# Second MoE of a fused attention and MoE kernel: early sums of x's quarters, results evacuated to any free slot, the last three in halves

## Chip, cores and metric

One core of one Trainium2 chip runs the whole program. The metric is device time in microseconds, the median of the runs shown; lower is better.

## What is computed

Three stages, each on the output of the one before, all in fp32:

```python
x = attention(q, k, v)                 # 4 x 8 x 576 x 64: downsampled (mean of 4) + banded local, added
x = x.transpose(0, 2, 1, 3).reshape(2304, 512)
h = np.maximum(x @ w_in, 0.0)          # MoE 1: 512 -> 2048 -> 512
x = (s * (h * h) + b) @ w_out
a, c = x @ w_a, x @ w_b                # MoE 2: 512 -> 1536 twice
out = (a * c) @ w_out2                 # 1536 -> 512
```

The change is in MoE 2, for the 2304 tokens that MoE 1 leaves in DRAM (`x2d`).

## The kernel before

Every fp32 operand of TensorE is split into a high and a low part (`hi`: ScalarE copies with rounding to float32r; `lo`: VectorE subtracts), and a product is three matmuls, hi x hi, hi x lo, lo x hi.

MoE 2 runs in three blocks of 768 tokens. A block holds its x transposed in one buffer (`x2`, one buffer, loaded by SyncE at L272) and works as seven products of a Strassen-like scheme on quarters of x (two of four 128-row groups by 384 tokens). The right-hand operands of the products are `B11, T2, B21, T1, T3, B22, T4`: four quarters of x and four sums of quarters, one of which (T3) takes the place of a quarter. `b_x` (L1173) makes them: it forms the sums in place, in the quarters' own memory (`step`, L1194, VectorE, 768 wide), and splits each operand into `xo` (hi L1200 on ScalarE, lo L1203 on VectorE). Because sums overwrite quarters, a sum waits until the operands that read the old content have been split, and the order is a fixed alternation of splits and sums:

```python
        split(0, (0, 0), x2)
        step((0, 1), (1, 1), (0, 1), ALU.subtract, x2)
        step((0, 0), (0, 1), (0, 0), ALU.add, [("xc", t, (0, 1)), ("xo", t, 0)])
```

The operands of the next block can be split only when the products of the last group of the block before have read the old ones. So the seven splits and the sums between them fall at the boundary of two blocks.

For each of six pairs of weight slices, a group computes both tensors' products (TensorE, L1326, `ab<-xo,w`: six 384-wide matmuls each), adds them up on VectorE (L1356, L1369, L1375, L1390, L1400) with one copy on ScalarE (L1350, L1363), and multiplies the two tensors (L1369, L1403) into `u`. `b_out` splits `u` into `gh` (L1442, ScalarE) and `gl` (L1445, VectorE) and multiplies it with the output weights: three 512-wide matmuls for each 128 tokens, hi x hi (L1466), hi x lo (L1467), lo x hi (L1468), into six banks `acc`, each filled over all of a block's groups. `b_comb` makes the weights' operands: hi/lo of slices (L1234, L1237), four sums (L1251), their split (L1268, L1272) and the last quarter's (L1279, L1282). `w_out` splits output weights (L439, L443).

`b_evac` (L1484) moves the six full banks out: ScalarE copies a bank to one of two `ev` buffers (L1490), SyncE writes it to `out` (L1494). With two buffers, an evacuation waits for the transfer of the one before last.

The order of the instructions is set by a planner (`Program.order`, L116 to 217): each task has an engine, an assumed duration, what it reads, the slots it needs (`acq`) and frees (`rel`), and a due time. The task that can start first goes next, and among equals the one due first:

```python
                    key = (s, t.due - t.lead, t.num)
                    if best is None or key < best[0]:
                        best = (key, t, picks, fs)
```

A due time passes backwards from a task to what it needs. `ANY` stands for either of two pools of 128 x 2 x 512 slots (`w`, 33 of them, and `wx`, 4), which weights, sums and temporaries share. A token, such as `("st",)`, limits how many slots one kind of task may hold. Each engine then runs its own instructions strictly in the order written.

Of the kernel before, what the change touches and what calls it, by code (L numbers as in the profile page):

```python
# [55 lines left out]
MAX_STAGED = 4  # L56
NU = max(BLOCKS[0] + 2, *BLOCKS, TN)
# [16 lines left out]
TOKENS = {"ca": 2, "cs": 2, "c2": 2, "st": 1, "wz": 2, "wo": 3, "tt": 6, "gt": 5}  # L74
# [153 lines left out]
def moe_chain(ctx, tc, qT, kT, vd, tq, tk, tv, qu, ku, vu, w_a1, w_o1, w_a2, w_b2, w_o2, sb, ident_d, bmask_d, emask_d, out):  # L228
# [322 lines left out]
    def down(b, hp, ph, pool_eng, v_eng, due=1e9):  # L551
# [170 lines left out]
    def tile_job(i, ph, due):  # L722
# [79 lines left out]
        def e_fn(p):  # L802
            sm = st["sm"] = pools[ph].tile([TQ, 2 * HP], F32, tag="tsm", name="tsm", bufs=3)
# [74 lines left out]
    def unit(u, due):  # L878
# [54 lines left out]
        def sb1(p):  # L933
            st["m"] = pools["b"].tile([128, 2, R], F32, tag="m", name="m", bufs=4)
# [241 lines left out]
    def b_x(t, after):  # L1176
# [31 lines left out]
        x2 = [("x2", t)]
        split(0, (0, 0), x2)
        step((0, 1), (1, 1), (0, 1), ALU.subtract, x2)  # L1210
        step((0, 0), (0, 1), (0, 0), ALU.add, [("xc", t, (0, 1)), ("xo", t, 0)])
        split(1, (0, 0), [("xc", t, (0, 0))])
        split(2, (1, 0), x2)
        step((1, 0), (1, 0), (0, 0), ALU.subtract, [("xc", t, (0, 0)), ("xo", t, 2)])
        P.made["xt1", t] = [last[0]]
        step((0, 0), (1, 1), (0, 0), ALU.subtract, [("xt1", t), ("xo", t, 1)])
        P.made["xt1", t] = [last[0]]
        split(3, (0, 0), [("xt1", t)])
        split(4, (0, 1), [("xc", t, (0, 1)), ("xt1", t)])
        split(5, (1, 1), [("xt1", t)])  # L1220
        split(6, (1, 0), [("xc", t, (1, 0)), ("xt1", t), ("xo", t, 3), ("xo", t, 4), ("xo", t, 5)], end=True)

    def b_comb(g, j):
# [21 lines left out]
        def add2(o, a, b, op):  # L1245
            def fn(picks):
# [4 lines left out]
                V.tensor_tensor(out=s[:, o * half:o * half + half], in0=x, in1=y, op=op)  # L1251
# [402 lines left out]
```

## Time and profile before

| | us |
|---|---|
| median of 3 runs | 943.24 (942.83 to 943.99) |
| profiled execution | 939.76 |
| its span (first to last work) | 937.6 |
| TensorE busy | 913.4 (97%) |
| VectorE busy | 790.3 (84%) |
| ScalarE busy | 498.5 (53%) |
| GpSimd busy | 69.2 (7%) |
| mean granted TensorE clock | 0.993 |

The span is the part of the profiled execution that the engines' records cover; 2.16 us lie around it. Matmuls overlap in the records, since one starts while the last one drains, so a TensorE that is 97% busy has little standstill but may still run at a reduced clock: the granted clock, 1.00 at full speed, tells of that. Each instruction has a start and a length; where the next one on the engine starts before that length is over, the distance of two starts is what an instruction costs. Square brackets at the end of a row give idle time of the engine just before it, and what ended it. MoE 2 fills the time from 505 us on.

### The profile page before, as it was taken

The page shows a single profiled execution, that of the slowest core. Times are in us where ns is not written, and L with a number is a line of the kernel's source. Part 1 is how long each engine was busy: PE and PEld are TensorE (multiplying, and loading weights), DVE is VectorE, ACT ScalarE, POOL GpSimd, SP SyncE. Part 2 cuts the span into 40 slices and gives each one's busy share as a digit, 9 for nine tenths or more (in the row PEclk, how much of TensorE's full clock was granted, in tenths as well). Part 3 has the DMA queues.
Part 4 walks back from the last instruction along what each step waited for, and adds up shares of the span by engine and source line. Part 5 has one row for each costly group of instructions (what it writes and reads, how often), then busy time and mean ns, then how long its engine had stood idle before and what let it go on. Part 6 is the DMA issues. An engine that isn't in the chain of part 4 may idle for free.

```text
span 937.6 us, 14356 instructions
## 1 busy us (share of the span) xinstructions
PE 913.4 (97%) x5319; PEld 847.1 (90%) x5319; DVE 790.3 (84%) x1385; ACT 498.5 (53%) x1144; POOL 69.2 (7%) x70
## 2 busy tenths in 40 slices
PE   8988999999999999999999999999999999999997
PEld 4668989998999999999999999998999998999996
DVE  6998998999999999995977998779877778877753
ACT  3999994445535444445987554335433335433322
POOL 2231201032222200000000000000000000000000
PEclk9998999999999999999999999999999999999999
DMA  7869626234354332304666331103100000300001
GB/s 207 239 180 348 148 72 205 71 102 127 113 103 123 108 88 74 110 15 175 208 213 251 120 113 46 45 23 135 46 23 23 23 23 12 102 31 16 1 1 68
DMA packets 46430, 96.75 MB, mean 103 GB/s; under 512 B 6344, under 2 KB 20520, under 8 KB 45976
## 3 DMA queue, kind: packets, MB, share of 16 engines
q1 hardware_dynamic: 39160, 93.16, 31.0%
q0 software_dynamic: 7200, 2.67, 2.4%
q8 instruction: 42, 0.69, 0.3%
q14 instruction: 28, 0.23, 0.1%
HBM read 83.22 MB, written 12.58 MB: 102 GB/s over the span
## 4 chain that ended last, share of the span: by engine, by line
PE 81%; DVE 8%; ACT 4%; issue 3%; DMA 2%; POOL 1%; SPq 0%; ACTq 0%; POOLq 0%
PE ab L1326 27%; PE acc L1095 6%; PE acc L1096 6%; PE acc L1097 6%; PE h L1052 6%; PE h L1053 6%; PE h L1054 6%; PE acc L1468 5%; PE acc L1467 5%; PE acc L1466 5%; DVE pr L962 1%; DMA pv<-in_vd_dram 1%; DVE xo L1203 1%; DMA tq<-in_bmask_dram 1%; ACT w L342 1%
## 5 line engine op out<-in xcount | busy, mean ns | idle before, releaser
L1326 PE MATMUL ab<-xo,w 128*128 128x384 f32 x1232 | 264.5, 339 | 0.8 <-DVE w L1356 0.5
L1326 PEld LDWEIGHTS ab<-xo,w 128*128 128x128 f32 x1232 | 222.8, 189 | 15.3 <-DVE u L1400 1.0
L1095 PE MATMUL acc<-gh,w 128*128 128x384 f32 (+1 forms) x384 | 134.0, 349 | 4.0 <-ACT w L809 2.0
L1052 PE MATMUL h<-xsh,w 128*128 128x384 f32 x384 | 131.0, 341 | 0.0
L1096 PE MATMUL acc<-gl,w 128*128 128x384 f32 x384 | 130.9, 341 | 0.0
L1097 PE MATMUL acc<-gh,w 128*128 128x384 f32 (+1 forms) x384 | 130.5, 340 | 0.0
L1053 PE MATMUL h<-xsl,w 128*128 128x384 f32 x384 | 128.9, 336 | 0.0
L1054 PE MATMUL h<-xsh,w 128*128 128x384 f32 x384 | 128.9, 336 | 0.0
L1069 ACT ACTIVATE u<-h 128x384 f32<-128x384 f32 x96 | 47.1, 491 | 115.8 <-PE h L1054 114.4
L1442 ACT ACTIVATE gh<-u 128x384 fp32r<-128x384 f32 x68 | 35.7, 525 | 93.4 <-DVE u L1403 58.4
L1095 PEld LDWEIGHTS acc<-gh,w 128*128 128x128 f32 x384 | 73.0, 190 | 8.1 <-ACT w L809 2.6
L1326 PE MATMUL ab<-xo,wx 128*128 128x384 f32 x280 | 77.5, 339 | 0.4 <-DVE u L1369 0.4
L1052 PEld LDWEIGHTS h<-xsh,w 128*128 128x128 f32 x384 | 72.1, 188 | 2.4 <-issue 2.0
L1096 PEld LDWEIGHTS acc<-gl,w 128*128 128x128 f32 x384 | 73.0, 190 | 0.6 <-DVE gl L1080 0.5
L1097 PEld LDWEIGHTS acc<-gh,w 128*128 128x128 f32 x384 | 72.9, 190 | 0.0
L1053 PEld LDWEIGHTS h<-xsl,w 128*128 128x128 f32 x384 | 72.2, 188 | 0.0
L1054 PEld LDWEIGHTS h<-xsh,w 128*128 128x128 f32 x384 | 72.1, 188 | 0.0
L1080 DVE TENSOR_TENSOR gl<-u,gh 128x384 fp32r<-128x384 f32 x96 | 54.4, 566 | 15.2 <-ACT gh L1076 14.9
L1350 ACT ACTIVATE w<-ab 128x384 f32<-128x384 f32 x30 | 14.7, 490 | 91.9 <-PE ab L1326 91.7
L1468 PE MATMUL acc<-w,gl 128*128 128x512 f32 x159 | 62.6, 394 | 0.0
L1467 PE MATMUL acc<-w,gh 128*128 128x512 f32 x159 | 62.6, 393 | 0.0
L1466 PE MATMUL acc<-w,gh 128*128 128x512 f32 x159 | 62.4, 393 | 0.0
(199 smaller groups left out, 1754.3 us busy)
## 6 DMA issues: line engine op xcount, KB each, us to landing
w<-in_w_o_dram SPq DMA_DIRECT2D x28, 512.0 KB
w<-in_w_a_dram SPq DMA_DIRECT2D x25, 512.0 KB
bk<-in_ku_dram SPq DMA_DIRECT2D x22, 320.0 KB
bk<-in_vu_dram SPq DMA_DIRECT2D x22, 320.0 KB
w<-wod SPq DMA_DIRECT2D x12, 512.0 KB
w<-in_w_b_dram SPq DMA_DIRECT2D x11, 512.0 KB
x2d<-ev SPq DMA_DIRECT2D x24, 192.0 KB
x<-x2d SPq DMA_DIRECT2D x3, 1536.0 KB
```

Source lines behind the costliest of these rows:

```text
L1052: nc.tensor.matmul(out=st["h"], lhsT=w[:, 0, k], rhs=hi[:, k], start=(k == 0), stop=False)
L1053: nc.tensor.matmul(out=st["h"], lhsT=w[:, 0, k], rhs=lo[:, k], start=False, stop=False)
L1054: nc.tensor.matmul(out=st["h"], lhsT=w[:, 1, k], rhs=hi[:, k], start=False, stop=(k == HP - 1))
L1069: A_.activation(out=st["u"], in_=st["h"], func=ACTF.Relu)
L1080: V.tensor_tensor(out=st["lo"], in0=st["u"], in1=st["hi"][:, :n].bitcast(F32), op=ALU.subtract)
L1095: nc.tensor.matmul(out=acc, lhsT=wh, rhs=st["hi"], start=(f == 0), stop=False)
L1096: nc.tensor.matmul(out=acc[:, :n], lhsT=wh, rhs=st["lo"], start=False, stop=False)
L1097: nc.tensor.matmul(out=acc, lhsT=wl, rhs=st["hi"], start=False, stop=(f == FA - 1))
L1326: nc.tensor.matmul(out=o, lhsT=w[:, k], rhs=x, start=(not more and k + n == 0), stop=(k == 1 and n == 2), skip_group_check=more,)
L1466: nc.tensor.matmul(out=acc, lhsT=gh, rhs=w[:, 0], start=first, stop=False)
L1467: nc.tensor.matmul(out=acc, lhsT=gh, rhs=w[:, 1], start=False, stop=False)
L1468: nc.tensor.matmul(out=acc, lhsT=gl, rhs=w[:, 0], start=False, stop=last)
```

## The change

First, six small buffers of the attention (`nb`, `sm`, `tnb`, `tsm` and `m` twice) have twice as many copies. Second, the sums of x's quarters: T1, T2 and T4 get slots of their own from `ANY` (a token `xt` allows three), and T3 alone is still made in place. So the sums no longer wait for splits. All are due 15 us ahead of the block, where before they had no due time of their own. Each split names the sums that must be done before its quarter may be given back, and the x buffer is given back when the four quarters that are operands have been split. All sums and all low parts remain on VectorE (`T_ENG`, `X2_ENG`, `S_ENG` name the engine of each). Third, evacuation: a full bank goes to any free slot (token `eva` allows four) in place of the two `ev` buffers. The last block's last three tiles go in halves of 256 columns: ScalarE copies half 0 and SyncE writes it out; VectorE copies half 1 and the DMA for it is issued by ScalarE.

```diff
-TOKENS = {"ca": 2, "cs": 2, "c2": 2, "st": 1, "wz": 2, "wo": 3, "tt": 6, "gt": 5}
+TOKENS = {"ca": 2, "cs": 2, "c2": 2, "st": 1, "wz": 2, "wo": 3, "tt": 6, "gt": 5, "xt": 3, "eva": 4}
...
-            nb = st["nb"] = pools[ph].tile([HK, 4], F32, tag="nb", name="nb", bufs=4)
+            nb = st["nb"] = pools[ph].tile([HK, 4], F32, tag="nb", name="nb", bufs=8)
...
         def step(out, a, b, op, reads):
+
             def fn(p):
-                V.tensor_tensor(out=q(*out), in0=q(*a), in1=q(*b), op=op)
-
-            last[0] = add("DVE", dve(2 * TN), fn, reads, [("xc", t, out)])
...
+                if isinstance(out, str):
+                    st[out] = slot(p[0], F32)
+                eng.tensor_tensor(out=q(out), in0=q(a), in1=q(b), op=op)
+
+            held[out] = add(
+                name, cost(2 * TN), fn, x2 + reads, [("xc", t, out)], [ANY, ("xt",)] if isinstance(out, str) else (), due=due - 15
+            )
+
+        step("T1", (0, 1), (0, 0), ALU.subtract, [])
+        step((0, 1), (1, 1), (0, 1), ALU.subtract, [("xc", t, "T1")])
+        step("T2", (0, 1), (0, 0), ALU.add, [("xc", t, (0, 1))])
+        step("T4", (1, 0), "T2", ALU.subtract, [("xc", t, "T2")])
+        done = []
+        for o, src in enumerate(((0, 0), "T2", (1, 0), "T1", (0, 1), (1, 1), "T4")):
...
+            tl = add(lo_name, lo_cost(2 * TN), lo, [("xh", t, o)], [("xo", t, o)])
+            if isinstance(src, str):
+                tl.rel = [pick(held[src], 0), "xt"]
+            else:
+                done.append(tl)
...
+        add("CTL", 0.0, free_fn, after=done, rel=["xx2"])
...
-        for tt in (3, 4, 5, 0, 1, 2):
-            sv = {}
-
-            def e_fn(p, tt=tt, sv=sv):
-                sv["ev"] = new("", "ev", [128, DM])
-                A_.activation(out=sv["ev"], in_=mm["bacc", t, tt], func=ACTF.Copy)
...
+        for n, tt in enumerate((3, 4, 5, 0, 1, 2)):
+            end = t == len(BLOCKS_B) - 1 and n > 2
             due = target_b((t + 1) * NP, 1.2)
...
+            halves = 2 if end else 1
...
+                    if i:
+                        V.tensor_copy(out=sv["ev"], in_=src)
+                    else:
+                        A_.activation(out=sv["ev"], in_=src, func=ACTF.Copy)
...
+                    (A_ if i else nc.sync).dma_start(out=out[r0:r0 + 128, i * w:i * w + w], in_=sv["ev"])
...
+                te = add(
+                    "DVE" if i else "ACT", dve(w) if i else act(w, True), e_fn, [("bacc", t, tt)], [("bev", t, tt, i)],
+                    [ANY, ("eva",)], (), due,
+                )
+                add("ACT" if i else "SP", 0.1 if i else 0.73, s_fn, [("bev", t, tt, i)], rel=[pick(te, 0), "eva"], due=due, seen=2.2)
```

With longer code ahead of them, the lines of MoE 2 have other numbers now: sums L1209 (L1194 before), splits L1224 and L1227 (L1200, L1203), weight sums L1271, weight low parts L1257 and L1293 (L1237, L1272), product sums L1377, L1390, L1396, L1411, L1421 (L1356, L1369, L1375, L1390, L1400), multiply L1424 (L1403), `gl` L1466 (L1445), output weights L450 (L443), evacuation L1520 and L1522, its DMA L1526.

**Boundary of block 0 to 1, VectorE.** `gl` and `u` belong to block 0's last groups, `xo` are the operands of block 1 (`xo_5060` is T1's, `xo_5061` T3's, `xo_5793` or `xo_5799` B22's, the next one T4's). Before:

```order
L1400 TENSOR_TENSOR u_7065<-w_7007,ab_7051 128x384
L1194 TENSOR_TENSOR x2_5847<-x2_5847 128x2x384
L1403 TENSOR_TENSOR u_7065<-u_7065,w_6965 128x384
L1194 TENSOR_TENSOR x2_5847<-x2_5847 128x2x384
L443 TENSOR_TENSOR w_7038<-w_6645,w_7038 128x512
L443 TENSOR_TENSOR w_7087<-w_6853,w_7087 128x512
L1445 TENSOR_TENSOR gl_7091<-u_7065,gh_7090 128x384
L1203 TENSOR_TENSOR xo_5060<-x2_5847,xo_5060 128x768
L1203 TENSOR_TENSOR xo_5061<-x2_5847,xo_5061 128x768
L1203 TENSOR_TENSOR xo_5799<-x2_5847,xo_5799 128x768
L1400 TENSOR_TENSOR u_7123<-w_7007,ab_7011 128x384
```

Now:

```order
L1466 TENSOR_TENSOR gl_7060<-u_7051,gh_7059 128x384
L450 TENSOR_TENSOR wx_7049<-w_6655,wx_7049 128x512
L1421 TENSOR_TENSOR u_7077<-w_7017,ab_7064 128x384
L1227 TENSOR_TENSOR xo_5060<-w_5948,xo_5060 128x768
L1424 TENSOR_TENSOR u_7077<-u_7077,w_6975 128x384
L1227 TENSOR_TENSOR xo_5061<-x2_5849,xo_5061 128x768
L1227 TENSOR_TENSOR xo_5793<-x2_5849,xo_5793 128x768
L450 TENSOR_TENSOR w_7100<-w_6863,w_7100 128x512
L1466 TENSOR_TENSOR gl_7104<-u_7077,gh_7103 128x384
L1421 TENSOR_TENSOR u_7122<-w_7017,ab_7021 128x384
```

The two L1194 sums are gone from between the splits (a third one, ahead of these rows, too), the splits of T1, T3 and B22 lie between the product sums, and the last product sum (L1400, now L1421) has only one `gl` and one output weight between it and the last of them.

**Boundary of block 1 to 2, VectorE.** The same kind of names, one block on (`u_8384` before is `u_8397` now). Before:

```order
L1194 TENSOR_TENSOR x2_7142<-x2_7142 128x2x384
L1403 TENSOR_TENSOR u_8341<-u_8341,w_8239 128x384
L1194 TENSOR_TENSOR x2_7142<-x2_7142 128x2x384
L443 TENSOR_TENSOR w_8363<-w_8126,w_8363 128x512
L1445 TENSOR_TENSOR gl_8367<-u_8341,gh_8366 128x384
L1400 TENSOR_TENSOR u_8384<-wx_8281,ab_8285 128x384
L1203 TENSOR_TENSOR xo_5060<-x2_7142,xo_5060 128x768
L1203 TENSOR_TENSOR xo_5061<-x2_7142,xo_5061 128x768
L1203 TENSOR_TENSOR xo_5799<-x2_7142,xo_5799 128x768
L1403 TENSOR_TENSOR u_8384<-u_8384,w_8217 128x384
L1237 TENSOR_TENSOR w_8332<-wx_5145,w_8332 128x512
L1272 TENSOR_TENSOR w_8414<-w_8274,w_8354 128x1024
```

Now:

```order
L1227 TENSOR_TENSOR xo_5060<-w_7196,xo_5060 128x768
L1424 TENSOR_TENSOR u_8356<-u_8356,w_8252 128x384
L1227 TENSOR_TENSOR xo_5061<-x2_7112,xo_5061 128x768
L1227 TENSOR_TENSOR xo_5793<-x2_7112,xo_5793 128x768
L450 TENSOR_TENSOR w_8377<-w_8139,w_8377 128x512
L1466 TENSOR_TENSOR gl_8381<-u_8356,gh_8380 128x384
L1421 TENSOR_TENSOR u_8397<-wx_8294,ab_8298 128x384
L1257 TENSOR_TENSOR w_8331<-w_5216,w_8331 128x512
L1227 TENSOR_TENSOR xo_5794<-w_7277,xo_5794 128x768
L1424 TENSOR_TENSOR u_8397<-u_8397,w_8230 128x384
L1293 TENSOR_TENSOR w_8417<-w_8287,w_8386 128x1024
L1466 TENSOR_TENSOR gl_8422<-u_8397,gh_8421 128x384
```

Two sums and one split that lay ahead of the multiply (L1403 of `u_8384`, now L1424 of `u_8397`) are no longer there; T4's split and a weight's low part stand ahead of it in their place.

**The end, ScalarE and VectorE**, with what each instruction waits for (an engine or a DMA queue). `acc` are the six banks. ScalarE before:

```order
L1490 ACTIVATE ev_9639<-acc_8661 128x512 [waits DMAHW4_49,PE_49]
L1490 ACTIVATE ev_9644<-acc_8685 128x512 [waits DMAHW5_49,PE_49]
L1490 ACTIVATE ev_9657<-acc_8697 128x512 [waits DMAHW1_49,PE_49,Activation_49]
L1490 ACTIVATE ev_9660<-acc_8604 128x512 [waits DMAHW2_49,PE_49,Activation_49]
L1490 ACTIVATE ev_9663<-acc_8624 128x512 [waits DMAHW3_49,PE_49,Activation_49]
L1490 ACTIVATE ev_9666<-acc_8633 128x512 [waits DMAHW4_49,PE_49,Activation_49]
```

ScalarE now:

```order
L1522 ACTIVATE wx_9649<-acc_8671 128x512 [waits PE_49]
L1522 ACTIVATE wx_9654<-acc_8695 128x512 [waits PE_49]
L1522 ACTIVATE w_9660<-acc_8707 128x512 [waits PE_49]
L1522 ACTIVATE w_9666<-acc_8616 128x256 [waits PE_49]
L1526 DMA out_0_dram<-w_9673 128x256 [waits DMAHW4_49,DVE_49]
L1522 ACTIVATE wx_9676<-acc_8635 128x256 [waits DMAHW1_49,PE_49,Activation_49]
L1526 DMA out_0_dram<-wx_9679 128x256 [waits DVE_49]
L1522 ACTIVATE wx_9682<-acc_8643 128x256 [waits PE_49]
L1526 DMA out_0_dram<-wx_9685 128x256 [waits DVE_49]
```

VectorE now:

```order
L1424 TENSOR_TENSOR u_9621<-u_9621,w_9510 128x384 [waits DVE_49]
L1466 TENSOR_TENSOR wx_9631<-u_9621,wx_9631 128x384 [waits Activation_49]
L1520 COPY w_9673<-acc_8616 128x256 [waits Activation_49]
L1520 COPY wx_9679<-acc_8635 128x256 [waits DVE_49,PE_49,Activation_49]
L1520 COPY wx_9685<-acc_8643 128x256 [waits DMAHW2_49,Activation_49]
```

Of the evacuations only two halves wait for a DMA queue now: their slots are those of the first two tiles. A copy of a half on VectorE waits for ScalarE, and each DMA on ScalarE's own row waits for VectorE and stands ahead of ScalarE's next half.

## Rows read from the trace of the kernel before

**Rows 1.** The page, busy time of each engine (share of the span) and instructions.

```profile
PE 913.4 (97%) x5319; PEld 847.1 (90%) x5319; DVE 790.3 (84%) x1385; ACT 498.5 (53%) x1144; POOL 69.2 (7%) x70
```

**Rows 2.** What TensorE waited for, 500 to 938 us: total, times, longest us.

```profile
PE acc L1468 <- DVE gl L1445: 1.6, 1, 1.6
...
PE ab L1326 <- DVE w L1356: 0.5, 1, 0.5
```

**Rows 3.** TensorE timeline, boundary 0 to 1: start us, length us, line, count.

```profile
641.66 0.39 PE L1467 MATMUL acc<-w,gh 128*128 128x512 f32 x1
...
642.59 0.40 PE L1468 MATMUL acc<-w,gl 128*128 128x512 f32 x1
...
646.02 0.39 PE L1466 MATMUL acc<-wx,gh 128*128 128x512 f32 x1
```

**Rows 4.** VectorE timeline, the same boundary.

```profile
637.52 0.95 DVE L1194 TENSOR_TENSOR x<-x 128x768 f32<-128x768 f32 x1
...
642.67 0.54 DVE L1400 TENSOR_TENSOR u<-w,ab 128x384 f32<-128x384 f32 x1
...
650.82 0.68 DVE L1237 TENSOR_TENSOR w<-w 128x512 fp32r<-128x512 f32 x1
...
653.03 0.95 DVE L1194 TENSOR_TENSOR x<-x 128x768 f32<-128x768 f32 x1
```

**Rows 5.** SyncE timeline, the same boundary: the load of block 2's x.

```profile
645.18 0.32 SPq L272 DMA_DIRECT2D x<-x2d  x1
```

**Rows 6.** TensorE timeline, boundary 1 to 2.

```profile
784.63 0.40 PE L1468 MATMUL acc<-w,gl 128*128 128x512 f32 x1
...
788.20 1.01 PE L1326 MATMUL ab<-xo,w 128*128 128x384 f32 x2
...
792.24 0.33 PE L1326 MATMUL ab<-xo,wx 128*128 128x384 f32 x1
792.41 0.51 PE L1326 MATMUL ab<-xo,w 128*128 128x384 f32 x2
```

**Rows 7.** VectorE timeline, the same boundary.

```profile
781.44 2.69 DVE L1203 TENSOR_TENSOR xo<-x,xo 128x768 fp32r<-128x768 f32 x3
784.05 0.56 DVE L1403 TENSOR_TENSOR u<-u,w 128x384 f32<-128x384 f32 x1
784.52 0.69 DVE L1237 TENSOR_TENSOR w<-wx,w 128x512 fp32r<-128x512 f32 x1
785.12 1.22 DVE L1272 TENSOR_TENSOR w<-w 128x1024 fp32r<-128x1024 f32 x1
```

**Rows 8.** Windows: busy PE, PEld, DVE, ACT, POOL; clock; DMA share; GB/s.

```profile
550.00:560.00 10.00, 10.00 (x53) 9.26 (x52) 9.86 (x21) 3.99 (x9) 0.00 (x0) 1.00 0.37 114
...
780.00:790.00 10.00, 8.03 (x33) 6.22 (x32) 9.95 (x17) 5.13 (x9) 0.00 (x0) 0.90 0.02 8
```

**Rows 9.** ScalarE timeline, the end.

```profile
927.65 1.30 ACT L1490 ACTIVATE ev<-acc 128x512 f32<-128x512 f32 x2 [2.81 <-PE acc L1468]
930.40 1.32 ACT L1490 ACTIVATE ev<-acc 128x512 f32<-128x512 f32 x2 [1.45 <-PE acc L1468]
933.22 1.29 ACT L1490 ACTIVATE ev<-acc 128x512 f32<-128x512 f32 x2 [1.50 <-DMA out_dram<-ev]
```

**Rows 10.** TensorE timeline, the end: the last matmul.

```profile
930.67 0.39 PE L1468 MATMUL acc<-wx 128*128 128x512 f32 x1
```

**Rows 11.** Chain that ended last, the end: one transfer (start us, us, what).

```profile
931.02 2.09 DMA out_dram<-ev
```

**Rows 12.** Chain within 30 to 60 us: GpSimd's DMA issue, a transfer of it.

```profile
32.32 1.20 POOL pv L544
...
42.29 6.99 DMA pv<-in_vd_dram
```

**Rows 13.** Groups of instructions by line: busy us, mean ns of one, idle before.

```profile
L1251 DVE TENSOR_TENSOR w<-w 128x256 f32<-128x256 f32 x88 | 35.3, 420 | 0.0
...
L1279 ACT ACTIVATE w<-w 128x256 fp32r<-128x256 f32 x29 | 11.7, 404 | 0.0
```

More of the change, by code (lines that the diff above doesn't have):

```diff
@@ L792, in m_fn @@
         def m_fn(p):
-            nb = st["nb"] = pools[ph].tile([TQ, 2 * HP], F32, tag="tnb", name="tnb", bufs=3)
+            nb = st["nb"] = pools[ph].tile([TQ, 2 * HP], F32, tag="tnb", name="tnb", bufs=6)
             for h in range(2):
@@ L1185, in b_x, with q @@
         load(src, 128 * HP * n * 4, [("x2d", t)], [("x2", t)], [("xx2",)], due=due - 25, after=after)
-        def q(i, j):
+        def q(src):
+            if isinstance(src, str):
+                return st[src].rearrange("p a m -> p (a m)")[:, :2 * TN].rearrange("p (a b) -> p a b", b=TN)
+            i, j = src
             return st["x"][:, 2 * i:2 * i + 2, j * TN:j * TN + TN]
-        last = [None]
+        x2 = [("x2", t)]
+        name, eng, cost = ENG[T_ENG]
+        held = {}
         def step(out, a, b, op, reads):
@@ L1208, in b_x @@
[L1208 to L1217, printed above, removed]
@@ L1250, in fn @@
                 x, y = (s[:, e * half:e * half + half] if isinstance(e, int) else quarter(*e) for e in (a, b))
-                V.tensor_tensor(out=s[:, o * half:o * half + half], in0=x, in1=y, op=op)
+                s_eng.tensor_tensor(out=s[:, o * half:o * half + half], in0=x, in1=y, op=op)
             return fn
+        s_name, s_eng, s_cost = ENG[S_ENG[j]]
         steps = [
-            (0.33, add2(0, (1, 0), (1, 1), ALU.add)), (0.33, add2(1, 0, (0, 0), ALU.subtract)),
-            (0.33, add2(2, (0, 0), (1, 0), ALU.subtract)), (0.33, add2(3, (0, 1), 1, ALU.subtract)),
+            add2(0, (1, 0), (1, 1), ALU.add), add2(1, 0, (0, 0), ALU.subtract), add2(2, (0, 0), (1, 0), ALU.subtract),
+            add2(3, (0, 1), 1, ALU.subtract),
         ]
         ts = None
-        for n, (dur, fn) in enumerate(steps):
-            ts = add("DVE", dur, fn, [("zt", p, j)], [("cs0", g, j)] if n == 3 else [], [ANY, ("st",)] if n == 0 else (), after=[ts] if ts else ())
+        for n, fn in enumerate(steps):
+            ts = add(s_name, s_cost(half), fn, [("zt", p, j)], [("cs0", g, j)] if n == 3 else [], [ANY, ("st",)] if n == 0 else (), after=[ts] if ts else ())
             if n == 0:
@@ L1484, in b_evac, with e_fn, s_fn @@
     def b_evac(t):
[L1485 to L1498 removed]
+        for n, tt in enumerate((3, 4, 5, 0, 1, 2)):
+            end = t == len(BLOCKS_B) - 1 and n > 2
+            due = target_b((t + 1) * NP, 1.2)
+            halves = 2 if end else 1
+            w = DM // halves
+            evs = []
+            for i in range(halves):
+                sv = {}
+                def e_fn(p, tt=tt, sv=sv, i=i, w=w):
+                    sv["ev"] = slot(p[0], F32)[:, 0, :w]
+                    src = mm["bacc", t, tt][:, i * w:i * w + w]
+                    if i:
+                        V.tensor_copy(out=sv["ev"], in_=src)
+                    else:
+                        A_.activation(out=sv["ev"], in_=src, func=ACTF.Copy)
+                def s_fn(p, tt=tt, sv=sv, i=i, w=w):
+                    r0 = starts_b[t] + tt * 128
+                    (A_ if i else nc.sync).dma_start(out=out[r0:r0 + 128, i * w:i * w + w], in_=sv["ev"])
[4 more added lines that the diff above has]
+                add("ACT" if i else "SP", 0.1 if i else 0.73, s_fn, [("bev", t, tt, i)], rel=[pick(te, 0), "eva"], due=due, seen=2.2)
+                evs.append(te)
+            if halves == 1:
+                release(evs[0], [pick(mm["bpick", t, tt], 0)])
     P.made["open", "r"] = []
```

37 lines of the change are left out of this document (18 added, 19 removed).

## Prediction

> **What bounds the kernel now.** I read the page's busy times first: TensorE is busy for 97% of the span [rows 1], so time can come only from the few places where it stands still or runs at the lower clock. The list of its waits in the second MoE names them [rows 2]: the longest is 1.6 us for a low half `gl` (L1445), and 0.5 us goes to a `w` (L1356). VectorE makes both. By TensorE's timeline nearly all of it lies at the two boundaries between blocks [rows 3, 6].
>
> At boundary 0 to 1 [rows 3], the step of a 512-wide matmul is (642.59 - 641.66) / 4 = 0.23 us; that of a 384-wide one is 0.17 (792.24 to 792.41 in [rows 6]). From 642.59 to 646.02 there are four wide steps and a product of six narrow ones, 0.93 + 1.03 = 1.96 us; 3.43 passed, so 1.47 is lost. The 0.5 for `w` comes behind it: 2.0 us.
>
> At boundary 1 to 2 [rows 6], from 784.63 to 788.20 there are four wide steps, 0.93 us, and 3.57 passed: 2.64 lost. Then the 14 product matmuls from 788.20 to 792.24 take 4.04 us where 14 x 0.173 = 2.4 is due: 1.6 lost, with nothing waited for. There the windows view has a granted clock of 0.90 [rows 8], a mean of 2.4 GHz and of some microseconds at 1.2 GHz, and TensorE had just stood still. This boundary costs 4.25 us.
>
> VectorE's own timeline says why it is late: around both boundaries it has no gap (9.95 of 10 us busy in 780 to 790 [rows 8]), and three 768-wide instructions on the next block's operands, 0.87 us from start to start, lie right ahead of what TensorE waits for [rows 4, 7].
>
> The end is the third place. The last matmul is done at 930.67 + 0.39 = 931.06 [rows 10], the span at 937.6. ScalarE evacuates six tiles as three pairs, from 927.65, 930.40 and 933.22 [rows 9]. The row puts the second pair's wait down to TensorE, but a bank fills every 3 x 0.23 = 0.7 us, so the third one was full near 929.0. What came at 930.4 is the first tile's transfer, 2.09 us long [rows 11], which frees one of two buffers. The third pair's 1.50 us is put down to a transfer openly.
>
> **The change, part by part.** *Doubled small buffers in the attention:* the order of VectorE and its waits are the same there. Cost and gain 0.
>
> *The sums, boundary 0 to 1.* The twelve sums stay on VectorE, so none of their 12 x 0.87 us is saved. But three of a block's four no longer lie among the operand splits: two stand in the order shown, the third ahead of it. So the `L1400` at 642.67 (now L1421) comes 3 x 0.87 = 2.6 us earlier, at 640.06. The 1.47 us lost behind it is less than that, and goes. The `w` of 650.1 lies ahead of all moved sums in the new order, so its 0.5 should go too; with the load below so near, I count half. Gain 1.7, between 0.7 (half of the 1.47 stays) and 2.0.
>
> *Boundary 1 to 2.* The steps by [rows 7] are 0.47 us (384-wide, 784.05 to 784.52), 0.60 (512-wide, 784.52 to 785.12), 0.87 (768-wide, 2.61 / 3). Two sums and one split less lie ahead of the multiply (L1403, now L1424): where three splits ran from 781.44, one 512-wide and one 768-wide run now. It starts at 781.44 + 0.60 + 0.87 = 782.9 in place of 784.05. Only `sl`, 1024-wide, is between it and `gl`; I take 1.14, on the line through the other steps. `gl` then starts at 782.9 + 0.47 + 1.14 = 784.5 and is done near 785.1. Undisturbed, TensorE wants it three wide steps after 784.63, at 785.3. The standstill goes with 0.2 us to spare, and I expect the clock not to fall without it. Gain 4.25 less 0.15 for so thin a margin: 4.1. If the margin fails by half a microsecond and the clock falls all the same, 4.25 - 0.5 - 1.6 = 2.1 is left, the lower bound.
>
> *Where the sums go.* In block 0, three sums of 0.87, 2.6 us, enter the stretch from 531 to 560. VectorE is 9.86 of 10 us busy at its end, but TensorE is at 10.00 there [rows 8] and waits for nothing: VectorE runs ahead by a margin that no row gives. I cost them at 0, bounded by 2.6. Block 2's come between 647 and 656, when VectorE is 2.6 us less behind than before; after them it is where it was. Cost 0.
>
> The first of block 2's sums waits for that block's load, and what VectorE does next is queued behind it. In the kernel before, the load is issued at 645.18 [rows 5] and its first user behind the boundary is the sum at 653.03 [rows 4], so it lands within 7.85 us. In the new order the last split that reads the buffer (`xo_5793`) has only a 512-wide and a 384-wide instruction between it and the L1421 of 640.06, so it ends near 640.06 - 0.47 - 0.60 = 639.0. The load then lands by 646.9; the sum has the place of the L1237 at 650.82 [rows 4], with 2.6 us of sums and one 512-wide instruction (0.60) less ahead of it: 647.6. Cost 0.
>
> *Evacuation to any slot.* The first three of the last six tiles no longer wait: they start at 927.65, 928.35, 929.05. ScalarE is free at 929.70, when the fourth bank is full. In the earlier blocks nothing waits for an evacuation [rows 2]: 0.
>
> *Halves through two queues.* In the order, VectorE's copy waits for ScalarE's half of the same bank, and ScalarE's next evacuation stands behind its DMA issue, which waits for VectorE's copy. The three tiles are one chain. (Two halves take the slots of the first two tiles and wait for their transfers, which by 2.09 us each end near 930.4 and 931.1, before the halves come.) A tile takes ScalarE's half (256-wide, 0.40), VectorE's (0.42) [rows 13], and an issue. No row has an issue on ScalarE; the nearest are SyncE's 0.32 [rows 5] and GpSimd's 1.20 [rows 12]. I take SyncE's, which belongs to the same kind of plain transfer. With 0.05 for each hand-over a tile is 1.2 us; the fourth starts at 929.74, the sixth at 932.15, and its copy ends at 933.0. Before, the last evacuation ended at 933.22 + 1.29 = 934.51 and the span 3.1 us behind it; half the bytes save about 0.3, so 933.0 + 2.8 = 935.8. Gain 1.8. At GpSimd's price three issues add 3 x 0.88 = 2.6, a loss of 0.8; with free issues the gain is 2.5.
>
> A rule speaks against the halves. The order shows that the two never run side by side. The Trainium skill's page "PSUM — Partial Sum Buffer", section "PSUM bank collisions raise a hardware error", has it that two engines collide on one bank and partitions even when both read, so software guards whole banks; no run here shows a collision. Were the halves side by side, the last would end near 931.5 in place of 933.0 and the time would be 1.5 us lower than forecast.
>
> *Sum:* 1.7 + 4.1 + 1.8 = 7.6 us. The profiled execution of 939.76 (span 937.6 and 2.16 around it) becomes 932.2. The median of the runs, 943.24, is 3.5 above that execution; I take the same gain from it: **935.6 us**, 0.8% faster. The bounds give 0.7 + 2.1 - 0.8 = 2.0 of gain at worst (941.2) and 2.0 + 4.25 + 2.5 = 8.75 at best (934.5), or 933.0 with 1.5 for halves side by side.
>
> **Rivals.**
>
> *A. The sums push elsewhere.* The 2.6 us in 531 to 560 find no room: TensorE stands still for them, and the clock falls once, 1.6 us as behind 788. For it: VectorE is busy for 9.86 of 10 us at the stretch's end [rows 8]. Against it: TensorE waits for nothing there now. Gain 7.6 - 4.2 = 3.4: 939.8.
>
> *B. The load becomes the wait.* Block 2's x lands at 653.0 as before, and its first sum holds VectorE's row for 5.4 us. TensorE has two products (2.1 us) in hand, loses 3.3, and 1.6 by the clock. Gain 7.6 - 4.9 = 2.7: 940.5. For it: the margin is 0.7 us. Against it: the load is issued some 6 us earlier, and nothing in its way is.
>
> *C. The transfers from ScalarE are slow, and the kernel slower.* If each of the three landed as GpSimd's `pv` did, 6.99 us behind its issue [rows 12], and one after the other, the end would be 930.6 + 3 x 7.0 + 1.4 = 953.0, 15.4 us later than now. Less 5.8 from the boundaries that is 9.6 slower: 952.8. It decides from 930.6 + 3L + 1.4 = 937.6 + 5.8 + 1.9, or L = 4.4 us. Against it: SyncE's out transfer took 2.09, and in the order no issue waits for the transfer before it. The Trainium skill (page "DMA: Bandwidth & Descriptors", section "Issuing engines are not separate DMA queues") says that all issuers share the same 16 engines; no trace here shows it for ScalarE.
>
> *D. The boundaries stay bound.* Another instruction, VectorE's or ScalarE's `gh`, becomes the last to arrive, and the clock falls as before. For it: the margin of 0.2 us. The 5.8 shrinks to 1 or less, with 0 to 0.8 from the end: 941.4 to 943.2.
>
> **How the numbers follow.** A measurement of this kernel can tell about 0.2%, 1.9 us, from no change. Chances: forecast 0.66, A 0.12, B 0.10, D 0.07, C 0.05. Forecast, A and B are faster by over 0.2% except where several bad ends meet, for which I take off 0.02: faster 0.86. Same is D and those, 0.09; slower is C, 0.05. The range goes from 933.0 (halves side by side) to 940.8, which holds A and B. Outside lie D, C and the worst ends, some 0.15.
>
> **What would show it.** Right: no TensorE wait of over 0.3 us at either boundary, a granted clock of 1.00 where it is 0.90, `L1421` at boundary 0 to 1 some 2.6 us earlier against TensorE's matmuls, three full evacuations with no wait for a transfer, and a span that ends 4.7 us behind the last matmul in place of 6.5. Wrong: a wait for a sum (L1209) or for the load near the start of block 2, a clock under 1.00 between 531 and 560, a ScalarE issue of over 1 us, or a last transfer of over 2.1 us.

## Result and the profile after

The changed kernel takes 933.92 us, median of 4 runs (933.25 to 935.82), against 943.62 (942.83 to 945.59) of the kernel before: ratio 0.9907, 95% interval 0.9879 to 0.9936, or 8.8 us less (6.0 to 11.4). The forecast was 935.6, in a range of 933.0 to 940.8. The profiled execution of the changed kernel took 934.12 us (span 932.3).

Its page, busy time of the engines, beside [rows 1]:

```profile
PE 913.2 (98%) x5319; PEld 847.0 (91%) x5319; DVE 789.9 (85%) x1388; ACT 497.4 (53%) x1144; POOL 69.7 (7%) x70
```

TensorE's busy time is what it was, in a span that is 5.3 us shorter. How much of the span belongs to the change is best read from MoE 2 alone, since the attention ahead of it varies from execution to execution. The first product and the last matmul of each kernel, from TensorE's timeline (start us, length us), first before, then after:

```profile
505.50 2.25 PE L1326 MATMUL ab<-xo,w 128*128 128x384 f32 x12
```

```profile
506.76 1.21 PE L1347 MATMUL ab<-xo,wx 128*128 128x384 f32 x6
```

```profile
926.29 0.39 PE L1489 MATMUL acc<-wx 128*128 128x512 f32 x1
```

Before, MoE 2 took 931.06 [rows 10] - 505.50 = 425.56 us from the start of its first product to the end of its last matmul, and the span went on for 6.5. After, it takes 926.68 - 506.76 = 419.92, and the span goes on for 5.6. So the change is worth 5.64 us inside MoE 2 and 0.9 at its end, 6.5 together. Where the 5.64 lie shows when the matmuls of the two traces are counted off from the first product: the 700th starts equally late in both (134.1 us), the 1100th 1.9 us earlier after the change, the 1500th 5.7 us earlier, and no more is gained from there on. The first step is boundary 0 to 1, the second boundary 1 to 2. MoE 2 began 1.3 us later in this execution than in the one before, which is the rest of the span's difference.

**The boundaries.** What TensorE waited for from 500 us on is one row now:

```profile
PE ab L1347 <- DVE u L1390: 0.4, 1, 0.4
```

The `gl` and `w` of [rows 2] are gone. The wait that is left lies near 521 us, at neither boundary, and the kernel before had it too (0.4 us for `u` L1369). The windows beside [rows 8], and the one of boundary 0 to 1:

```profile
550.00:560.00 10.00, 10.00 (x54) 9.29 (x53) 9.98 (x20) 3.62 (x7) 0.00 (x0) 1.00 0.33 97
...
640.00:650.00 10.00, 10.00 (x50) 8.51 (x49) 9.95 (x20) 5.17 (x10) 0.00 (x0) 1.00 0.52 184
...
780.00:790.00 10.00, 10.00 (x51) 8.73 (x50) 9.40 (x20) 5.54 (x11) 0.00 (x0) 1.00 0.07 27
```

TensorE is busy without a gap, the granted clock is 1.00 in all three, and VectorE has no reserve in 550 to 560 (9.98 of 10 us, 9.86 before); the three sums moved to this part of block 0 start at 533.76, 558.17 and 561.65. Boundary 1 to 2 in VectorE's timeline, beside [rows 7], and in TensorE's, beside [rows 6]:

```profile
780.87 0.69 DVE L1257 TENSOR_TENSOR w<-w 128x512 fp32r<-128x512 f32 x1
781.47 0.95 DVE L1227 TENSOR_TENSOR xo<-w,xo 128x768 fp32r<-128x768 f32 x1
782.34 0.56 DVE L1424 TENSOR_TENSOR u<-u,w 128x384 f32<-128x384 f32 x1
782.81 1.22 DVE L1293 TENSOR_TENSOR w<-w 128x1024 fp32r<-128x1024 f32 x1
784.01 0.56 DVE L1466 TENSOR_TENSOR gl<-u,gh 128x384 fp32r<-128x384 f32 x1
```

```profile
784.73 0.40 PE L1489 MATMUL acc<-wx,gl 128*128 128x512 f32 x1
785.09 4.11 PE L1347 MATMUL ab<-xo,w 128*128 128x384 f32 x21
```

One 512-wide and one 768-wide instruction stand ahead of the multiply at 782.34, then `sl`, then `gl`, as foreseen. `gl` ends at 784.57, and TensorE takes it at 784.73: 0.16 us to spare. Boundary 0 to 1:

```profile
641.27 0.55 DVE L1421 TENSOR_TENSOR u<-w,ab 128x384 f32<-128x384 f32 x1
...
648.97 0.95 DVE L1209 TENSOR_TENSOR w<-x 128x768 f32<-128x768 f32 x1
```

```profile
640.32 0.32 SPq L278 DMA_DIRECT2D x<-x2d  x1
```

Counted from the first product, `L1421` starts at 641.27 - 506.76 = 134.51 us; the `L1400` of [rows 4] started at 642.67 - 505.50 = 137.17. That is 2.66 earlier. Block 2's load [rows 5] is issued 6.1 us earlier by the same count, and its first sum (648.97) has no idle time ahead of it.

**The end.** ScalarE's timeline beside [rows 9], then VectorE's (ACTq is a DMA issue in ScalarE's row):

```profile
923.25 1.29 ACT L1522 ACTIVATE wx<-acc 128x512 f32<-128x512 f32 x2 [2.80 <-PE acc L1489]
924.63 1.08 ACT L1522 ACTIVATE w<-acc 128x512 f32<-128x512 f32 x2
926.20 0.38 ACTq L1526 DMA_DIRECT2D out_dram<-w  x1
926.71 0.38 ACT L1522 ACTIVATE wx<-acc 128x256 f32<-128x256 f32 x1 [1.00 <-PE acc L1489]
927.58 0.34 ACTq L1526 DMA_DIRECT2D out_dram<-wx  x1
927.97 0.38 ACT L1522 ACTIVATE wx<-acc 128x256 f32<-128x256 f32 x1 [0.88 <-DVE wx L1520]
928.84 0.34 ACTq L1526 DMA_DIRECT2D out_dram<-wx  x1
```

```profile
925.75 0.43 DVE L1520 COPY w<-acc 128x256 f32<-128x256 f32 x1 [4.71 <-ACT w L1522]
927.13 0.42 DVE L1520 COPY wx<-acc 128x256 f32<-128x256 f32 x1 [0.95 <-ACT wx L1522]
928.38 0.42 DVE L1520 COPY wx<-acc 128x256 f32<-128x256 f32 x1 [0.83 <-ACT wx L1522]
```

Three whole tiles and the fourth's half run without a wait for a transfer. From then on it is a chain: ScalarE's half 926.71, VectorE's 927.13, the issue 927.58, the next half 927.97. That is 1.26 us a tile, while a bank fills in 0.7. The row at 926.71 puts its 1.00 us of idle time down to TensorE, but that bank was full near 926.0; ScalarE had the DMA issue in its row until 926.58. (This half also takes the slot of the first whole tile and waits for its transfer. A first tile's slot came free 2.1 us after its copy in the kernel before, 928.3 to 930.4; from 923.9 that gives 926.0, so the transfer was not what came last.) The last matmul was over at 926.68; the last copy ends 2.1 us behind it, and the span 3.5 us behind the copy.

### The profile page after: what moved, and what is told of

It reads as the page before. It is cut to its first block, busy times and chain, and to the rows that moved or that the text cites. A ratio compares the mean times of both kernels' runs of the same rounds, so it can differ in the third digit from the quotient of the medians.

```text
span 932.3 us, 14367 instructions
## 1 busy us (share of the span) xinstructions
PE 913.2 (98%) x5319; PEld 847.0 (91%) x5319; DVE 789.9 (85%) x1388; ACT 497.4 (53%) x1144; POOL 69.7 (7%) x70
## 4 chain that ended last, share of the span: by engine, by line
PE 84%; DVE 5%; ACT 4%; issue 3%; DMA 2%; POOL 1%; SPq 0%; ACTq 0%
PE ab L1347 28%; PE acc L1102 7%; PE acc L1103 6%; PE h L1059 6%; PE acc L1104 6%; PE h L1061 6%; PE h L1060 6%; PE acc L1488 5%; PE acc L1489 5%; PE acc L1487 5%; DVE pr L969 1%; DMA pv<-in_vd_dram 1%; ACT z L342 1%; DMA tq<-in_bmask_dram 1%; ACT w L378 1%
## 5 line engine op out<-in xcount | busy, mean ns | idle before, releaser
L1347 PE MATMUL ab<-xo,w 128*128 128x384 f32 x1376 | 273.7, 338 | 0.4 <-DVE u L1390 0.4
L1347 PEld LDWEIGHTS ab<-xo,w 128*128 128x128 f32 x1376 | 246.1, 188 | 16.3 <-DVE u L1390 0.7
L1489 PE MATMUL acc<-w,gl 128*128 128x512 f32 x138 | 54.4, 394 | 0.0
L1488 PE MATMUL acc<-w,gh 128*128 128x512 f32 x138 | 54.3, 394 | 0.0
L1487 PE MATMUL acc<-w,gh 128*128 128x512 f32 x138 | 54.2, 393 | 0.0
L354 DVE TENSOR_SCALAR w<-w 128x512 uint16<-128x512 f32 x61 | 45.6, 767 | 8.3 <-ACT w L349 8.0
```

The source lines that it names most:

```text
L1347: nc.tensor.matmul(out=o, lhsT=w[:, k], rhs=x, start=(not more and k + n == 0), stop=(k == 1 and n == 2), skip_group_check=more,)
L1487: nc.tensor.matmul(out=acc, lhsT=gh, rhs=w[:, 0], start=first, stop=False)
L1488: nc.tensor.matmul(out=acc, lhsT=gh, rhs=w[:, 1], start=False, stop=False)
L1489: nc.tensor.matmul(out=acc, lhsT=gl, rhs=w[:, 0], start=False, stop=last)
```

## Experiments

M is the time from MoE 2's first product to the end of its last matmul, E from there to the end of the span, both from one profiled execution each, read as above.

| kernel | M us | E us | M + E against before | ratio of the runs |
|---|---|---|---|---|
| before | 425.56 | 6.5 | | |
| changed | 419.92 | 5.6 | -6.5 | 0.9907 (0.9879 to 0.9936) |
| changed, once more | 419.92 | 5.6 | -6.5 | 0.9927 (0.9904 to 0.9951) |
| sums only | 419.82 | 6.5 | -5.8 | 0.9956 (0.9936 to 0.9976) |
| evacuation only, whole tiles | 425.60 | 3.8 | -2.7 | 0.9973 (0.9948 to 0.9997) |
| small buffers only | 425.32 | 6.5 | -0.2 | 0.9992 (0.9967 to 1.0016) |
| changed, no halves | 419.89 | 3.8 | -8.4 | 0.9912 (0.9879 to 0.9946) |
| the same, once more | 419.91 | 3.7 | -8.4 | 0.9903 (0.9867 to 0.9938) |
| changed, halves all issued by SyncE | 419.82 | 4.8 | -7.4 | |
| changed, one more split | 420.79 | | | |
| three more splits, and again | 422.81, 422.84 | | | |
| delay in two pieces | 424.21 | | | |
| five more splits | 425.69 | | | |

The start of MoE 2 lay between 504.46 and 511.48 us in these executions, and it does not follow the change: two executions of one kernel with three more splits began it at 507.44 and 507.68, two of the changed kernel at 506.76 and 509.01. That is a large part of the spread of the runs, and why M and E say more here than a median. E is known to 0.1 us, as the span is.

**Sums only.** The kernel before with the change's `b_x` and the token `xt`:

```diff
-TOKENS = {"ca": 2, "cs": 2, "c2": 2, "st": 1, "wz": 2, "wo": 3, "tt": 6, "gt": 5}
+TOKENS = {"ca": 2, "cs": 2, "c2": 2, "st": 1, "wz": 2, "wo": 3, "tt": 6, "gt": 5, "xt": 3}
...
+                if isinstance(out, str):
+                    st[out] = slot(p[0], F32)
+                eng.tensor_tensor(out=q(out), in0=q(a), in1=q(b), op=op)
```

> The kernel before with the sums in slots of their own, and nothing else of the change. Theory (VectorE's row at the two boundaries is what TensorE waited for): TensorE's standstill at both boundaries and the fall of the clock behind 788 us go, 5.7 us in all, and the end stays as it was (6.5 us from the last matmul to the end of the span): about 938. Rival (free banks and slots of the evacuation opened the boundaries): waits for gl stay, 942 or more.

What TensorE waited for in it, from 495 us:

```profile
PE ab L1342 <- DVE u L1385: 0.4, 1, 0.4
```

M falls by 5.74 and E stays. The sums' own slots are the whole gain at the boundaries; the rival, free banks, has no part in it.

**Evacuation only.** The kernel before with the change's `b_evac` and the token `eva`, all tiles whole (the edit against the changed kernel's `b_evac`):

```diff
-            end = t == len(BLOCKS_B) - 1 and n > 2
+            end = False
```

> The kernel before with full tiles evacuated to any slot, no halves, sums as before. Theory: the six evacuations at the end follow the banks without a wait, the last copy ends 0.65 us after the last matmul and the span 3.1 to 3.5 us after that, 3.8 to 4.2 in place of 6.5: 2.5 us less; the boundaries still stand still for over a microsecond each and the granted clock still falls: about 941. Rival (the evacuation opened the boundaries): no wait of TensorE over 0.3 us there, 936 or less.

```profile
PE acc L1468 <- DVE gl L1445: 1.6, 1, 1.6
```

The boundaries are as before, with the same `gl` as in [rows 2], and E is 3.8. Any slot in place of two buffers is worth 2.7 us, all at the end.

**Small buffers only.** The kernel before with the six doubled `bufs=`.

> The kernel before with the doubled small buffers of the attention alone. Theory: same order, same waits, no difference: 943.6 within 1 us. Rival (the measured 8.8 us hold a part from the attention that the second MoE's 6.6 us do not explain): about 941.5, and the attention's stretch up to the second MoE shorter by 2 us.

M + E differs by 0.2, but these buffers lie ahead of MoE 2. There, MoE 2 began at 507.94 us in this kernel's profiled execution and at 505.50 in the one before, so that stretch was not shorter. The runs do not tell the kernel from before (0.9992, with an interval that leaves room for about 3 us either way). That the 8.8 us of the first measurement hold a part from the attention is thus not shown, and not excluded. None is needed: the interval reaches down to 6.0, and the second measurement gives 0.73% of 942.31, 6.9 us.

**No halves.** The changed kernel with the edit `end = False` above.

> The changed kernel with its last three tiles evacuated whole by ScalarE and written by SyncE. Theory (the halves are a chain of 1.26 us a tile, slower than the banks fill, and a half transfer is no shorter): the last copy ends 0.65 us after the last matmul in place of 2.1, the span 3.1 to 3.5 after it, so 1.5 to 1.9 us less than the changed kernel: about 932.2. Rival (halves through two queues save time): 0.5 to 1 us more than the changed kernel.

ScalarE's and SyncE's timelines at its end:

```profile
922.79 1.99 ACT L1522 ACTIVATE w<-acc 128x512 f32<-128x512 f32 x3
924.92 0.60 ACT L1522 ACTIVATE wx<-acc 128x512 f32<-128x512 f32 x1
```

```profile
925.54 0.33 SPq L1526 DMA_DIRECT2D out_dram<-wx  x1
```

ScalarE follows the banks, and the last copy ends at 925.52, 0.7 us behind the last matmul (924.84). SyncE's last issue is over at 925.87 and the span ends 2.7 us later. E is 1.9 shorter than with halves: of the 2.7 us that any slot is worth, the halves give 1.9 back.

> The changed kernel with whole tiles at the end, once more. Theory: 3.74 us from the last matmul to the end of the span, 1.9 less than with halves; 8.5 us less than before between MoE 2's first product and the end, about 0.9% in the runs. Rival (the end of the span hides it): no difference to the changed kernel.

The second execution has the same M and E within 0.1. In the runs the two kernels' intervals against before overlap (0.9903 and 0.9912 without, 0.9907 and 0.9927 with halves), so the gain of 1.9 us over the changed kernel is shown by the traces and only fits the runs. By M + E it is the best version here.

The changed kernel was run once more, on another chip than the runs without halves:

> The changed kernel once more, beside the one without halves on the same chip. Theory: 5.66 us from the last matmul to the end of the span, 419.9 us from MoE 2's first product to its last matmul. No rival.

Its M is 419.92 again, and E 5.6.

**Halves all issued by SyncE.** The changed kernel with

```diff
-                    (A_ if i else nc.sync).dma_start(out=out[r0:r0 + 128, i * w:i * w + w], in_=sv["ev"])
+                    nc.sync.dma_start(out=out[r0:r0 + 128, i * w:i * w + w], in_=sv["ev"])
...
-                add("ACT" if i else "SP", 0.1 if i else 0.73, s_fn, [("bev", t, tt, i)], rel=[pick(te, 0), "eva"], due=due, seen=2.2)
+                add("SP", 0.73, s_fn, [("bev", t, tt, i)], rel=[pick(te, 0), "eva"], due=due, seen=2.2)
```

> The changed kernel with SyncE issuing the DMAs of VectorE's halves too, so that ScalarE's row holds only evacuations. Theory (ScalarE's issue, which waits for VectorE, makes the chain): ScalarE's three halves follow the banks, the last copy ends 0.9 us after the last matmul in place of 2.1, SyncE's sixth issue 0.4 after it: the span ends about 4.5 us after the last matmul in place of 5.66, and 0.7 later than with whole tiles. Rival (the turn between the two engines on a bank alone makes it): 5.3 or more.

```profile
927.12 0.38 ACT L1522 ACTIVATE w<-acc 128x256 f32<-128x256 f32 x1 [0.31 <-PE acc L1489]
927.87 0.38 ACT L1522 ACTIVATE wx<-acc 128x256 f32<-128x256 f32 x1 [0.37 <-PE acc L1489]
```

```profile
928.28 0.42 DVE L1520 COPY wx<-acc 128x256 f32<-128x256 f32 x1 [0.33 <-ACT wx L1522]
```

```profile
928.28 1.63 SPq L1526 DMA_DIRECT2D out_dram<-wx  x3
```

E is 4.8, between the two expectations. ScalarE's halves do follow the banks (the last starts 0.1 behind the last matmul at 927.77), and the last copy ends at 928.70, 0.9 behind it. So the wait for VectorE in ScalarE's own row made most of the chain. But now SyncE has six half issues, of which the last three take 1.63 us, and its last one is over at 929.91, 1.2 us after the copy. From there it is 2.7 us to the end, the same as for whole tiles. In the changed kernel the last issue, ScalarE's, is over at 928.84 + 0.34 = 929.18, and 3.1 us pass to the end.

What these 2.7 and 3.1 us consist of is in SyncE's row. Its last instructions (the last line of the program, L1677 here) wait for the DMA queues one after the other. Those from the last transfer's landing on, in the kernel without halves, with halves issued by SyncE, and in the changed kernel (line, instruction, count, ns, first and last start):

```profile
L1677 SPq EVENT_SEMAPHORE  x4: 17/22/28, 927.6 to 928.5; - x4
L1677 SPq EVENT_SEMAPHORE  x9: 17/28/28, 931.3 to 932.6; - x9
L1677 SPq EVENT_SEMAPHORE  x9: 17/28/28, 930.7 to 932.3; - x9
```

A whole tile landed at 927.6, 1.7 us behind the end of its issue (925.9); half a tile after 1.4 us (929.9 to 931.3) when SyncE issued it and after 1.5 us (929.2 to 930.7) when ScalarE did. So half the bytes did save 0.2 to 0.3 us, against the theory of the runs above that a half transfer is no shorter. What took the saving back lies behind the landing: 1.0 us to the end of the span with whole tiles, 1.3 and 1.6 with halves. With whole tiles the last transfer's queue stands near the end of SyncE's list, and four instructions are left: two waits of the list and two behind it. With halves it stands near the front, and nine are left: seven and two. What follows the list takes the same 0.8 us in all three (from 927.75, 931.78 and 931.50), so the whole difference lies in the list. The kernel before and the one with the evacuation only have the same four, and 1.0 us. Why the list of the changed kernel takes 0.3 us longer than that of the kernel with SyncE's issues is not shown; its last transfer, ScalarE's, landed only 0.1 us later behind its issue.

**One more split.** The changed kernel, with the low part of T4's split in block 2 done twice, so that one more 768-wide VectorE instruction stands ahead of the multiply at boundary 1 to 2 (`range(4)` and `range(6)` for three and five more):

```diff
+                for _ in range(2 if t == 2 and o == 6 else 1):
-                lo_eng.tensor_tensor(out=xo[o][:, 2:4], in0=q(src), in1=xo[o][:, 0:2].bitcast(F32), op=ALU.subtract)
+                    lo_eng.tensor_tensor(out=xo[o][:, 2:4], in0=q(src), in1=xo[o][:, 0:2].bitcast(F32), op=ALU.subtract)
```

> The changed kernel with block 2's T4 split done twice by VectorE, one more 768-wide instruction (0.87 us) ahead of the multiply at boundary 1 to 2; the order is otherwise the same. Theory (gl is done 0.16 us before TensorE wants it): TensorE stands still there for about 0.7 us, once, and the granted clock stays at 1.00. Rival 1 (VectorE's row is not what bounds the boundary): nothing lost. Rival 2 (any standstill there brings the clock down): 0.7 and 1.6, 2.3 us lost.

```profile
789.14 0.50 PE L1488 MATMUL acc<-wx,gh 128*128 128x512 f32 x1
...
790.19 0.50 PE L1490 MATMUL acc<-wx,gl 128*128 128x512 f32 x1 [0.31 <-DVE gl L1467]
```

```profile
780.00:790.00 10.00, 9.81 (x46) 7.98 (x44) 9.96 (x16) 5.63 (x9) 0.00 (x0) 1.00 0.00 0
```

M is 0.87 longer, the whole of the added instruction: `gh` comes late as well, which takes the little that `gl` had to spare. VectorE's row bounds this boundary still. The clock stays at 1.00.

**Three more splits.**

> The same with the split done four times, three more 768-wide instructions, 2.6 us, as many as the change took away there. Theory: TensorE stands still for about 2.45 us and the granted clock falls behind it, 1.6 more: 4.0 us, as in the kernel before. Rival (it was another part of the change that kept the clock up): 2.45 us lost and the granted clock at 1.00.

```profile
784.68 0.40 PE L1490 MATMUL acc<-wx,gl 128*128 128x512 f32 x1
787.13 0.50 PE L1488 MATMUL acc<-wx,gh 128*128 128x512 f32 x1 [2.05 <-ACT gh L1464]
...
788.18 0.50 PE L1490 MATMUL acc<-wx,gl 128*128 128x512 f32 x1 [0.31 <-DVE gl L1467]
788.64 8.81 PE L1348 MATMUL ab<-xo,w 128*128 128x384 f32 x48
```

```profile
785.00:790.00 5.00, 2.63 (x12) 1.84 (x12) 4.96 (x11) 1.64 (x3) 0.00 (x0) 1.00 0.00 0
790.00:795.00 5.00, 5.00 (x29) 4.76 (x28) 3.84 (x9) 2.28 (x5) 0.00 (x0) 1.00 0.14 54
```

From 784.68 to 788.64 four wide steps, 0.93 us, are due and 3.96 pass: 3.0 us of standstill, somewhat more than the 2.64 of the kernel before. Yet the granted clock stays at 1.00, and M is 2.89 longer, not 4. The theory falls: TensorE's standstill there does not by itself bring the clock down.

**The same once more, and the delay in two pieces.** The second has one more split ahead of the multiply and one and a half more `sl` behind it:

```diff
+            late = (g, j) == (12, 1)
+            for _ in range(2 if late else 1):
...
+            if late:
+                V.tensor_tensor(out=st["s"][:, 0], in0=st["sum"][:, 0], in1=st["sh"][:, 0].bitcast(F32), op=ALU.subtract)
```

> The kernel with three more splits once more. Theory 1 (the same standstill has the same effect in each execution): 2.9 us lost and a granted clock of 1.00 again. Theory 2 (it depends on when the standstill falls, which the attention's length shifts from run to run): the clock may fall this time, 1 to 1.6 us more.

> The changed kernel with the delay at boundary 1 to 2 shaped as in the kernel before: one more split ahead of the multiply and 1.7 us more of the low part between the multiply and gl. TensorE should stand still for 0.35 us, run two matmuls, and stand still for 2.3, 2.65 in all. Theory 1 (the shape matters, two matmuls between two stops): the granted clock falls, 1.6 us more, 4.2 in all. Theory 2 (the shape does not matter; it fell in the kernels before and not with three more splits for another reason): 2.65 and a granted clock of 1.00.

The windows of the repeat, then TensorE's timeline and the windows of the two pieces:

```profile
785.00:790.00 5.00, 2.64 (x11) 1.56 (x10) 4.96 (x10) 1.35 (x3) 0.00 (x0) 1.00 0.00 0
790.00:795.00 5.00, 5.00 (x30) 4.76 (x29) 3.94 (x10) 2.56 (x5) 0.00 (x0) 1.00 0.14 54
```

```profile
784.64 0.40 PE L1494 MATMUL acc<-wx,gl 128*128 128x512 f32 x1
785.11 0.50 PE L1492 MATMUL acc<-wx,gh 128*128 128x512 f32 x1
785.45 0.40 PE L1493 MATMUL acc<-wx,gh 128*128 128x512 f32 x1
788.14 0.50 PE L1494 MATMUL acc<-wx,gl 128*128 128x512 f32 x1 [2.30 <-DVE gl L1471]
788.61 6.70 PE L1352 MATMUL ab<-xo,w 128*128 128x384 f32 x28
```

```profile
785.00:790.00 5.00, 2.63 (x11) 1.88 (x11) 4.93 (x10) 1.18 (x3) 0.00 (x0) 0.95 0.00 0
790.00:795.00 5.00, 5.00 (x23) 5.00 (x22) 3.02 (x8) 2.26 (x4) 0.00 (x0) 0.71 0.14 54
```

The repeat is as the first, M within 0.03. In two pieces, the standstill begins and ends within 0.05 us of where it did with three more splits, and is as long (784.64 to 788.61). Only the two matmuls in it come at its front and not near its end, and the granted clock falls to 0.95 and 0.71: M is 4.29 longer, 1.4 more than with the same standstill in the other shape. This is the shape of the kernel before, and in the three traced kernels that kept the old sums the clock fell (0.80 and 0.85 in 785 to 790 and 790 to 795 before, 0.85 and 0.81 with the evacuation only, 0.99 and 0.66 with the small buffers only).

**Five more splits.**

> Five more splits, 4.35 us ahead of the multiply. Both theories: TensorE stands still for 4.6 us. If the length of the standstill decides, the granted clock falls here, 1.6 us more, 6.2 in all; if it stays at 1.00, 4.6.

```profile
785.00:790.00 5.00, 3.59 (x10) 2.98 (x11) 4.43 (x11) 1.53 (x3) 0.00 (x0) 0.67 0.11 41
```

```profile
PE acc L1488 <- ACT gh L1464: 4.0, 1, 4.0
```

Here the clock falls too (0.67 in 785 to 790), behind a wait of 4.0 us, and M is 5.77 longer, between the two forecasts. A wait of 2.05 us left the clock up twice, and in the old shape it fell with a longest wait of 1.6 [rows 2]. So the length of the longest wait alone does not decide it. What does stays open. The two pieces ran once, and a rival is left: that the moment counts, not the shape (the repeat's theory 2). By the traces the clock fell at 788.0 us (before), 788.5 (evacuation only), 789.9 (small buffers only), 789.5 (two pieces) and 786.7 (five more splits), where the last matmul ahead of the standstill had begun at 784.6, 784.5, 787.1, 784.6 and 781.7: the fall keeps no fixed distance to the standstill. Two executions of one shape without a fall are too few to tell the two apart. A run that shifts the two matmuls in small steps through the same standstill, or the standstill as a whole, was not made.

## Why the prediction was right, and where not

The mechanism was right: inside MoE 2 the time came from the three places named, and from no other. The sum was 7.6 us; the traces give 6.5, and the missing 1.1 us are nearly all in the last term (below). That the median came out at 933.92, better than the 935.6 forecast, is luck: the measured 8.8 us carry the spread of what lies ahead of MoE 2, and the repeat gives 6.9.

- *Boundaries, 5.8 us forecast.* 5.64 measured: 1.9 at boundary 0 to 1 (1.7 forecast) and 3.8 at boundary 1 to 2 (4.1 forecast). `L1421` came 2.66 us earlier (2.6 forecast), `gl` was done near 784.6 with 0.16 us to spare (0.2 forecast), and of the 6.25 us that the two boundaries had cost 0.6 stays lost.
- *The clock, 1.6 us of it.* It did stay at 1.00. But the step "I expect the clock not to fall without it" rested on a standstill that brings the clock down, and three more splits show a longer one that does not. The 1.6 us were real in the kernel before (1.4 in the kernel with the delay in two pieces), but they cannot be counted on whenever 2.6 us of standstill are put in or taken out. Whether the pattern of standing and running or its moment decides is not shown.
- *Sums moved into 531 to 560 and 647 to 656, cost 0.* Right: TensorE waits for nothing there, though VectorE has 9.98 of 10 us busy in 550 to 560. Rival A had no case.
- *The load, cost 0.* Right: issued 6.1 us earlier, and the sum came without a wait. Rival B fell.
- *Doubled small buffers, 0.* Nothing speaks against it, but the runs leave room for about 3 us either way.
- *Evacuation to any slot.* The first tiles' waits went as forecast. That it is worth 2.7 us by itself, more than with halves, I had not worked out. (The 2.09 us of [rows 11] are those of a later tile's transfer, issued at 931.02; the first tile's, issued at 928.27, was over by the 930.4 that the reading gives it.)
- *Halves, 1.8 us forecast for the end, 0.9 measured.* The failed step is the last term, "933.0 + 2.8": the time from the last copy to the end of the span was 3.5 us. Half the bytes did save the 0.2 to 0.3 us, but the forecast left what lies behind the last transfer's landing as it was, 1.0 us, and it became 1.6, because SyncE's list of waits then had nine instructions left and not four. The chain itself was 1.26 us a tile against 1.2 forecast, 0.2 more on the last copy (2.1 us behind the last matmul in place of 1.9). The two, 0.7 and 0.2, make the missing 0.9.
- *The rule on PSUM banks.* The Trainium skill (page "PSUM — Partial Sum Buffer", section "PSUM bank collisions raise a hardware error") gives guarding whole banks as the simple form of its rule, and in the trace each half on VectorE starts about 0.04 us after ScalarE's half is over (926.71 + 0.38, then 927.13). Halves side by side were not tried, so no run shows what a collision would do.
- *Rival C.* The last transfer issued by ScalarE landed 1.9 us behind the start of its issue (928.84 to 930.7), far from the 4.4 that would have decided. An issue took 0.34 to 0.38 us of ScalarE's row, near SyncE's 0.32.

## To carry to other kernels

When an engine that is 84% busy delays the one that is 97% busy, look at its row at the few places where the busy one stops: three instructions of 0.87 us out of the way at two boundaries gave 5.6 us, 1.6 of it by the clock, with no work removed. A tile split over two engines must be shared without a turn: here the halves of one bank went one after the other, with a DMA issue in the same row, and cost 1.9 us over whole tiles on one engine that was fast enough to follow. What comes behind the last transfer is part of the price too: here it grew by 0.6 us when the last transfer's queue no longer stood near the end of SyncE's list of waits. Read a small change inside a long program between two events of its own stage, since the stages ahead vary more than the change.

## What had not been expected of the hardware

Two standstills of the same length at the same place (784.64 or 784.68 to 788.61 or 788.64 us) had different effects on TensorE's granted clock: 1.00 behind one, in two executions (784.97 to 788.93 in the second), and down to 0.71 behind the other, in one, with two 512-wide matmuls at the front of the standstill in place of near its end. And the program's end takes 2.7 us from the end of SyncE's last issue whether 128 or 256 KB are written, 3.1 from that of ScalarE's: the 0.2 to 0.3 us that the half transfer saves are spent behind its landing, in SyncE's list of waits.
